# Weight units split four units ahead of use, and a timetable of its own for the second expert's rows

## The chip, the cores and the metric

The kernel runs on one core of a Trainium2 chip. The metric is the device time of one execution in microseconds (us); of several executions the median is taken. TensorE (PE) multiplies matrices, VectorE (DVE) and ScalarE (ACT) work element by element, GpSimd (POOL) issues the gathers and scatters, and SyncE (SP) issues most of the other DMAs. Each engine runs its own program strictly in order, and so does each issuing queue: an instruction that waits holds up all that stand behind it on its engine.

## What is computed

The reference chains three stages. Attention is a retention: 8 batches, 8 heads, 576 tokens, head dimension 64, with scores multiplied by a decay. Its output, 4608 tokens of 512, goes through a mixture of 8 experts of which each token takes one, and the sum through an MLP with a squared ReLU.

```python
# attention
scores = scale * np.matmul(q, k.transpose(0, 1, 3, 2))
ret = scores * Dmat[None, :, :, :]
return np.matmul(ret, v)
...
# mixture of experts: w1[e] is 512 x 1024, w2[e] 1024 x 512
expert_idx = np.argmax(x @ w_gate, axis=1)
for e in range(E):
    mask = expert_idx == e
    h = np.maximum(x[mask] @ w1[e], 0.0)
    out[mask] = gate_w[mask, None] * (h @ w2[e])
...
# MLP: 512 -> 2048 -> 512
r = np.maximum(x @ w_in, 0.0)
return (r * r) @ w_out
```

## The kernel before

**Stages.** Attention runs over 36 tiles of 128 tokens to about 160 us. Then come the experts to about 600 us, and then the MLP, as products of Strassen's kind. The change lies in the stage of the experts.

**Units.** Every expert has 640 places for rows, in CT = 5 tiles of 128. Its hidden layer is cut into 8 slices of 128, and one slice of one expert is a unit: u = 8e + f, 64 units in all (NU). Products are made exact enough by splitting each operand into a high and a low half and adding three products: high by high, low by high, high by low. For a unit, `first(u)` multiplies the expert's rows (`xt`, two halves) by the slice of w1 into a PSUM tile `l` (L813 to L815; three buffers of `l1_ps`); `finish_part` makes from it hh, the high half of the ReLU, on ACT (L819) and hl, the low half, on DVE (L820). `second(u)` multiplies hh and hl by the slice of w2 into accumulators `acc` (L837 to L839). `first` has two parts. For expert 0 these are the lead (tiles 0 and 1, 256 columns, matrix `lead`) and the rest (384 columns); for the others columns 0 to 320 and 320 to 640, which the texts here call a and b. The lead part of units 0 to 5 (MORE = 6) and its `second` are worked off ahead of the loop. So units 0 to 5 are short there: three tiles, 384 columns.

**The loop.** For u from 0 to 63 the body issues loads and what else unit u has to do, then first(u + 1), then second(u). PE is thus one `first` ahead of its `second`. The order in which the calls stand in the body is the order on every engine; no scheduler moves anything.

**Weights.** `load_unit(v)` loads the 512 KB of a unit into `raw` (SP, L106; a pool `stg` of two buffers, so that a load waits until the split of two units before has read its raw). `split_unit(v)` makes the high half on ACT (L112) at once and returns a function that makes the low half on DVE (L114). In iteration u of before, unit u + 7 is loaded and unit u + 6 (AHEAD = 6) is split, near the start of the body.

**Rows of the next expert.** They are fetched tile by tile in four steps, each on its own engine: `gather` (POOL, into `row`, two buffers), `drop` (SP, L778, the tile to a DRAM buffer `r_d`), `lay` (SP, L783, four DMAs of 64 KB that read it back in another layout into `xs`) and `transp` (DVE transposes `xs` into `xf`, L793; ACT makes xt's high half, L797; DVE its low half, L798). A table gives for each step and tile the distance d at which it happens, where d = 0 is the first unit of the expert before: GATHER, DROP, LAY, TURN. Negative numbers reach into the unit group two experts before. For expert 1 there is no such group, so its first steps are written out by hand: gathers of tiles 0 and 1 ahead of the loop, drops of 0 and 1 and the gather of 2 in unit 0, the drop of 2 in unit 1.

**The jobs.** From unit 5 on most units carry a piece of the MLP's preparation (`work`). In `split_wide`, the kind that units 5 and 7 carry, `words` works on a loaded `craw` (SP, L128): ACT size (L141) and four DVE operations (L142 to L152). After the unit's `first` follow ACT cw (L177) and DVE L158, and at the start of the next unit `last_job` issues DVE L180 and L181, and the put, a DMA of 512 KB from cw to `ws_d` (SP, L182). In unit 5, `gate_of` (L295 to L301, five small DVE operations and one of ACT) stands between the two.

**Order in the body.** The load of raw, the load of craw, the end of the last job with its put, the split of u + 6 (high half; the low half is deferred into `rests`), then the steps of the next experts' rows (lay before drop before gather, logits, `transp` with its low half into `rests`), then one of `rests`, the job's `words`, the others of `rests`, then first(u + 1), the job's middle, second(u).

Of the kernel before, what the change touches and what calls it, by code (L numbers as in the profile page):

```python
# [26 lines left out]
FIN = 6  # L27
LEAD = 2
MORE = 6
GATHER, DROP, LAY, TURN = (-3, -2, -1, 1, 2), (-1, 0, 1, 3, 4), (0, 1, 2, 4, 5), (2, 3, 4, 5, 6)  # L30
TINY = 2.0 ** -15 * 1.125
GROUPS = [(0, 8), (8, 16), (16, 24), (24, 30), (30, 36)]

# [17 lines left out]
def body(ctx, tc, att, tab_v, tab_x, masks, wg, ident, pick, cst, wu, wd, out):  # L51
    nc = tc.nc
    vec, act, pe, pool, sp = nc.vector, nc.scalar, nc.tensor, nc.gpsimd, nc.sync
# [9 lines left out]
    w_a = scope(ctx, "w_a", 4, side="right")  # L63
# [40 lines left out]
    def load_unit(u, on=None):  # L104
        raw = on.tile([128, CT, 4, 128], F32, tag="xs", name="raw").rearrange("p a b c -> p (a b c)")[:, 0:1024] if on else pools["stg"].tile([128, 1024], F32, tag="raw", name="raw")
        sp.dma_start(out=raw, in_=wu[u])  # L106
        return raw

    def split_unit(u, raw, on):

        w = ring(u).tile([128, 2, 1024], F32R, tag="w", name="w")
        act.activation(out=w[:, 0], in_=raw, func=AF.Copy)  # L112
        w_q[u] = w
        return lambda: on.tensor_tensor(out=w[:, 1], in0=raw, in1=w[:, 0].bitcast(F32), op=ALU.subtract)  # L114
# [196 lines left out]
    def stream(on, n=None):  # L311

        n = len(ring_q) if n is None else n
        w = on.tile([128, 4, 2, 256], F32R, tag="w", name="wq")
        sp.dma_start(out=w.rearrange("p k s n -> p k (s n)").bitcast(F32), in_=ws_d[stream_of[n]])
        ring_q[n] = w
# [7 lines left out]
    with ExitStack() as es:  # L324
# [278 lines left out]
        raw = {}  # L603
# [89 lines left out]
    NU = NE * 8  # L693
# [56 lines left out]
    with ExitStack() as es:  # L750
# [6 lines left out]
        def gather(e, tiles):  # L757
            for i in tiles:
                j = CT * e + i
                if e == 0:  # L760
                    fetch_rows(xs_t[e][:, i].rearrange("p q c -> p (q c)"), x_d[:, :], gidx[:, j:j + 1])
                    continue
                whole[e, i] = row_p.tile([128, 512], F32, tag="row", name="row")
                fetch_rows(whole[e, i], x_d[:, :], gidx[:, j:j + 1])
# [11 lines left out]
        def drop(e, i):  # L776
            row = whole.pop((e, i))
            sp.dma_start(out=r_d[CT * e + i - CT], in_=row)  # L778
# [6 lines left out]
        def transp(e, i):  # L785
            xs = xs_t[e]
            hi, lo = [a[:, :, 128 * i:128 * i + 128] for a in xt_t[e]]
            if e == 0:
                src = acc_b.tile([128, 4, 128], F32, tag=f"acc{i}", name=f"acc{i}")
                turn_rows(src, xs[:, i].rearrange("p q c -> p (q c)"))  # L790
            else:
                src = xf_p.tile([128, 4, 128], F32, tag="xf", name="xf")
                vec.transpose(  # L793
                    out=src.rearrange("f k (t i) -> f k t i", i=32),
                    in_=xs[:, i].rearrange("q t (k j) -> q k t j", k=4),
                )
            act.activation(out=hi, in_=src, func=AF.Copy)  # L797
            return lambda: vec.tensor_tensor(out=lo, in0=src, in1=hi.bitcast(F32), op=ALU.subtract)  # L798
# [134 lines left out]
            )  # L933

        x0_t, x0_c = [], {}
        AHEAD = 6
        tiles = range(LEAD)
        first(0, (0,))
        fold()
# [46 lines left out]
        raw, made, wide, last_job = {}, [], [], None  # L986
# [19 lines left out]
                        totals += [("sum", work[u][1], r) for r in range(2)]  # L1006
                    break
        assert not ins and not outs and not totals
        raw[AHEAD] = load_unit(AHEAD)
        transp(0, 2)()  # L1010
        first(5, (0,))
        transp(0, 3)()
# [7 lines left out]
        for u in range(NU):  # L1020
            e, f = divmod(u, 8)
            v = u + AHEAD + 1
            if v < NU:
                raw[v] = load_unit(v)
            if u + 1 in work:
                what, j, r = work[u + 1]
                if what != "sum":
                    wide.append(load_wide(2 * j + r, 0 if what == "in" else 1))
            v = u + AHEAD
            job, rests = None, []  # L1030
            if last_job:
                f_ = next(last_job)
                if f_:
                    f_()
                last_job = None
            if v in raw:
                rests.append(split_unit(v, raw.pop(v), vec))
            if u in work:
                what, j, r = work[u]
                if what == "in":  # L1040
                    job = narrow(wide.pop(0), ("ca", "cb")[r], made)
                elif what == "sum":
                    job = left_factors(j, *made[2 * j:], r)
                else:
                    job = split_wide(2 * j + r, wide.pop(0))
            if v == NU + 2:
                assert not last_job and not wide
                early.close()
                w_d = scope(late_es, "w_d", 4, side="right", reuse="tile")
                x0_p = scope(late_es, "x0_p", 1, side="right", reuse="tile")  # L1050
            if v in (NU, NU + 1):
                stream(w_a, 4 + v - NU)
            if v >= NU + 2:
                stream(w_d, v - NU - 2)
            for n, d in ((e + 1, f), (e + 2, f - 8)):
                if n >= NE:
                    continue
                if n == 1 and d == 0:
                    drop(1, 0)
                    drop(1, 1)  # L1060
                    gather(1, [2])
                if n == 1 and d == 1:
                    drop(1, 2)
                if d == 0:
                    places_for(n)
                for i in range(CT):
                    if d == LAY[i]:
                        lay(n, i)
                    if d == DROP[i] and (n, i) in whole:
                        drop(n, i)  # L1070
                    if d == GATHER[i]:
                        gather(n, [i])
                if 1 <= d <= CT:
                    logit(n, d - 1)
                if d in TURN:
                    rests.append(transp(n, TURN.index(d)))
            for f_ in rests[:1]:
                f_()
            if job:
                next(job)  # L1080
            for f_ in rests[1:]:
                f_()
            if u == NU - 3:
                with tc.block():
                    tc.mark_branch_hint_location("rest", "LikelyTaken", [mybir.EngineType.PE])
            if u + 1 < NU:
                first(u + 1, (1,) if u + 1 < MORE else (0, 1))
            if f == 5:
                gate[e] = gate_of(sm, lg_t.pop(e), CT)
            if job:  # L1090
                next(job)
                last_job = job
            if u < NU - FIN:
                second(u, range(LEAD if u < MORE else 0, CT))
                if f == 7:
                    finish(e)
# [407 lines left out]
```

## Time and profile before

| what | us |
|---|---|
| median of 3 runs | 1361.5 (1359.88 to 1361.81) |
| the profiled execution's own time | 1361.44 |
| its span | 1359.7 |
| PE busy | 1340.3 |
| DVE, ACT, POOL busy | 832.9, 546.8, 257.8 |

The span is the stretch that the profiler's records cover, 1.7 us less than the time of the same execution. In the profile, "busy" is the time in which an engine executes, and the idle time ahead of an instruction is put down to whatever released it last. Granted clock is the speed at which PE was allowed to run, 1.00 for the full one. A unit of expert 1 takes PE about 6.9 us.

### The profile page before, as it was taken

What the parts mean: (1) busy time and instruction counts of PE and PEld (TensorE: products, weight loads), DVE (VectorE), ACT (ScalarE), POOL (GpSimd) and SP (SyncE); (2) the same over time, 40 slices, a digit from 0 to 9 for tenths busy, and PEclk for the clock granted to TensorE, in tenths of its full rate; (3) what the DMA queues carried; (4) which work ended last, traced back from release to release, by engine and by line L of the source; (5) the groups of instructions that cost most, each with busy time, mean ns of one, the idle gap of its engine ahead of it and who ended that gap; (6) DMA issues with size and microseconds to landing.
All of it is one profiled execution on the core that took longest, in us unless ns stands there. A gap on an engine that the chain in (4) does not pass through costs nothing.

```text
span 1359.7 us, 21532 instructions
## 1 busy us (share of the span) xinstructions
PE 1340.3 (99%) x8113; PEld 1154.0 (85%) x8113; DVE 832.9 (61%) x1510; ACT 546.8 (40%) x1064; POOL 257.8 (19%) x261
## 2 busy tenths in 40 slices
PE   8999999999999999999999999999999999999998
PEld 6888888999999999989888888888888888888887
DVE  5888757788797888727764563346633566244422
ACT  1232334454455554515544443344423444244321
POOL 2243252240432423112220030001300012000000
PEclk9999999999999999999999999999999999999999
DMA  9999668788978878576865666666656666565562
GB/s 348 350 341 324 198 180 270 257 274 264 302 262 281 283 240 281 194 268 237 294 239 199 226 226 216 216 224 197 243 208 234 209 227 228 203 217 194 191 233 103
DMA packets 129936, 329.10 MB, mean 242 GB/s; under 512 B 20382, under 2 KB 73630, under 8 KB 107808
## 3 DMA queue, kind: packets, MB, share of 16 engines
q1 hardware_dynamic: 121632, 306.51, 65.8%
q0 software_dynamic: 8192, 21.15, 5.3%
q8 instruction: 65, 1.06, 0.3%
q14 instruction: 47, 0.39, 0.1%
HBM read 266.89 MB, written 61.75 MB: 242 GB/s over the span
## 4 chain that ended last, share of the span: by engine, by line
PE 85%; issue 6%; DMA 5%; DVE 2%; SPq 1%; ACT 1%; POOL 1%; POOLq 0%; DVEq 0%; ACTq 0%
PE b L1168 24%; PE fa L1241 10%; PE fa L1240 10%; PE fa L1242 10%; PE l L813 4%; PE l L814 4%; PE l L815 4%; PE acc L837 4%; PE acc L838 4%; PE acc L839 4%; PE x L435 2%; PE sc L383 2%; PE x L431 2%; PE stp L407 1%; DMA idn<-ident 1%
## 5 line engine op out<-in xcount | busy, mean ns | idle before, releaser
L1168 PE MATMUL b<-xt,wq 128*128 128x512 f32 (+1 forms) x1296 | 264.8, 362 | 2.4 <-ACT xt L742 0.7
L1168 PEld LDWEIGHTS b<-xt,wq 128*128 128x128 f32 x1296 | 221.0, 188 | 41.3 <-ACT xt L742 1.1
L1240 PE MATMUL fa<-wq,ch 128*128 128x512 f32 x576 | 224.1, 389 | 0.0
L1242 PE MATMUL fa<-wq,cl 128*128 128x512 f32 x576 | 224.1, 389 | 0.0
L1241 PE MATMUL fa<-wq,ch 128*128 128x512 f32 x576 | 224.1, 389 | 0.0
L1230 DVE TENSOR_TENSOR cl<-g,ch 128x512 fp32r<-128x512 f32 (+1 forms) x160 | 108.6, 687 | 175.3 <-ACT ch L1229 172.9
L1229 ACT ACTIVATE ch<-g 128x512 fp32r<-128x512 f32 (+1 forms) x160 | 91.5, 584 | 183.5 <-PE fa L1241 183.5
L813 PE MATMUL l<-xt,w 128*128 128x320 f32 (+1 forms) x480 | 150.0, 313 | 2.3 <-DVE hl L820 2.3
L814 PE MATMUL l<-xt,w 128*128 128x320 f32 (+1 forms) x480 | 150.0, 312 | 0.0
L815 PE MATMUL l<-xt,w 128*128 128x320 f32 (+1 forms) x480 | 149.9, 312 | 0.0
L733 POOL TENSOR_TENSOR xsum<-yf 128x256 f32<-128x256 f32 x80 | 63.7, 805 | 452.4 <-DVE yf L721 388.7
L837 PE MATMUL acc<-w,hh 128*128 128x512 f32 x320 | 126.3, 395 | 1.3 <-ACT hh L819 1.1
L1242 PEld LDWEIGHTS fa<-wq,cl 128*128 128x128 f32 x576 | 108.1, 188 | 22.6 <-DVE cl L1230 0.2
L1240 PEld LDWEIGHTS fa<-wq,ch 128*128 128x128 f32 x576 | 108.1, 188 | 22.4
L1241 PEld LDWEIGHTS fa<-wq,ch 128*128 128x128 f32 x576 | 108.1, 188 | 22.4
L839 PE MATMUL acc<-w,hl 128*128 128x512 f32 x320 | 125.2, 391 | 0.7 <-DVE hl L820 0.7
L838 PE MATMUL acc<-w,hh 128*128 128x512 f32 x320 | 125.8, 393 | 0.0
L1154 ACT ACTIVATE s<-b 128x512 f32<-128x512 f32 (+1 forms) x120 | 66.5, 555 | 104.9 <-PE b L1168 104.9
L819 ACT ACTIVATE hh<-l 128x320 fp32r<-128x320 f32 (+2 forms) x128 | 54.5, 434 | 127.2 <-PE l L815 104.8
L1189 DVE TENSOR_TENSOR s<-s,s 128x512 f32<-128x512 f32 (+1 forms) x40 | 25.5, 638 | 113.6 <-ACT s L1154 113.6
L813 PEld LDWEIGHTS l<-xt,w 128*128 128x128 f32 x480 | 90.7, 189 | 5.0 <-DVE hl L820 2.5
L814 PEld LDWEIGHTS l<-xt,w 128*128 128x128 f32 x480 | 90.8, 189 | 2.5 <-DVE xt L798 0.2
(177 smaller groups left out, 2083.4 us busy)
## 6 DMA issues: line engine op xcount, KB each, us to landing
wq<-ws_d SPq DMA_DIRECT2D x142, 1024.0 KB
raw<-wu SPq DMA_DIRECT2D x62, 512.0 KB
in<-att SPq DMA_DIRECT2D x28, 1024.0 KB
craw<-wd SPq DMA_DIRECT2D x32, 512.0 KB
ws_d<-cw SPq DMA_DIRECT2D x24, 512.0 KB
x_d<-xr SPq DMA_DIRECT2D x72, 128.0 KB
r_d<-row SPq DMA_DIRECT2D x35, 256.0 KB
xs<-r_d SPq DMA_DIRECT2D x140, 64.0 KB
```

What stands on the lines that cost most here:

```text
L813: pe.matmul(ps, w[:, 0, k], hi[:, k, cs], start=(k == 0), stop=False)
L814: pe.matmul(ps, w[:, 0, k], lo[:, k, cs], start=False, stop=False)
L815: pe.matmul(ps, w[:, 1, k], hi[:, k, cs], start=False, stop=(k == 3))
L837: pe.matmul(acc[i], hh[:, cs], w[:, 0], start=(f == 0), stop=False)
L838: pe.matmul(acc[i], hh[:, cs], w[:, 1], start=False, stop=False)
L839: pe.matmul(acc[i], hl[:, cs], w[:, 0], start=False, stop=(f == 7))
L1168: pe.matmul(ps, w[:, a, c], xc[T][i, b][c], start=(i in (5, 1, 4) and m == 0), stop=(m == 5), skip_group_check=True,)
L1229: act.activation(out=hi[:, o], in_=s, func=AF.Copy)
L1230: vec.tensor_tensor(out=lo[:, o], in0=s, in1=hi[:, o].bitcast(F32), op=ALU.subtract)
L1240: pe.matmul(acc[i], hi[:, cs], w[:, 0], start=(f == 0), stop=False)
L1241: pe.matmul(acc[i], hi[:, cs], w[:, 1], start=False, stop=False)
L1242: pe.matmul(acc[i], lo[:, cs], w[:, 0], start=False, stop=(f == 15))
```

## The change

The four lists become a table STEPS with a row of lists for n = 1 (expert 1) and one with the old numbers for all the others. For expert 1 tiles 0 and 1 are still gathered ahead of the loop; the drops are at d = 0, 1, 2, 4, 5, the lays at 1, 2, 3, 5, 6 and the transposes at 3, 4, 5, 6, 7. The steps written out by hand for expert 1 go. AHEAD becomes 4: iteration u loads unit u + 5 and splits unit u + 4. The load ahead of the loop goes, and so do those of iteration 0, since units 0 to 5 have their weights by other ways (unit 5 among them). In iterations 1 to 4 (u + 1 < MORE) the split, with its low half at once, follows first(u + 1) instead of standing near the start; first(u + 1) and its hh and hl then stand ahead of it. From iteration 5 on it stands where it stood. The conditions near the end of the loop are written in u instead of v and mean the same units. No instruction is added or taken away. Lines of the changed kernel up to the loop have numbers 3 higher.

```diff
-GATHER, DROP, LAY, TURN = (-3, -2, -1, 1, 2), (-1, 0, 1, 3, 4), (0, 1, 2, 4, 5), (2, 3, 4, 5, 6)
+STEPS = {
+    1: ((-1, -1, 1, 2, 3), (0, 1, 2, 4, 5), (1, 2, 3, 5, 6), (3, 4, 5, 6, 7)),
+    2: ((-3, -2, -1, 1, 2), (-1, 0, 1, 3, 4), (0, 1, 2, 4, 5), (2, 3, 4, 5, 6)),
+}
...
-        AHEAD = 6
+        AHEAD = 4
...
-        raw[AHEAD] = load_unit(AHEAD)
...
             v = u + AHEAD + 1
-            if v < NU:
+            if 6 <= v < NU:
                 raw[v] = load_unit(v)
...
-            if v in raw:
+            if v in raw and u + 1 >= MORE:
                 rests.append(split_unit(v, raw.pop(v), vec))
...
             for n, d in ((e + 1, f), (e + 2, f - 8)):
                 if n >= NE:
                     continue
-                if n == 1 and d == 0:
-                    drop(1, 0)
-                    drop(1, 1)
-                    gather(1, [2])
-                if n == 1 and d == 1:
-                    drop(1, 2)
+                gathers, drops, lays, turns = STEPS[min(n, 2)]
...
-                    if d == LAY[i]:
+                    if d == lays[i]:
                         lay(n, i)
...
             if u + 1 < NU:
                 first(u + 1, (1,) if u + 1 < MORE else (0, 1))
+            if v in raw and u + 1 < MORE:
+                split_unit(v, raw.pop(v), vec)()
```

**SP's queue, units 1 to 7.** `raw<-wu` is a unit's load, `r_d<-row` a drop, `xs<-r_d` the four pieces of a lay, `craw<-wd` and `ws_d<-cw` the job's load and put. Before, from the drop of tile 3 to the second job's load:

```order
L778 DMA r_d<-row 128x512
L106 DMA raw<-wu 128x1024
L128 DMA craw<-wd 128x1024
L783 DMA xs<-r_d 32x4x128 x4
L778 DMA r_d<-row 128x512
L106 DMA raw<-wu 128x1024
L783 DMA xs<-r_d 32x4x128 x4
L106 DMA raw<-wu 128x1024
L128 DMA craw<-wd 128x1024
L182 DMA ws_d<-cw 128x1024
L106 DMA raw<-wu 128x1024
L128 DMA craw<-wd 128x1024
```

and in the changed kernel, from the first job's load on:

```order
L131 DMA craw<-wd 128x1024
L781 DMA r_d<-row 128x512
L109 DMA raw<-wu 128x1024
L786 DMA xs<-r_d 32x4x128 x4
L781 DMA r_d<-row 128x512
L109 DMA raw<-wu 128x1024
L131 DMA craw<-wd 128x1024
L185 DMA ws_d<-cw 128x1024
L786 DMA xs<-r_d 32x4x128 x4
L109 DMA raw<-wu 128x1024
L131 DMA craw<-wd 128x1024
```

The last `xs<-r_d`, that of tile 4, stood ahead of the put with two loads between, and stands right behind it now.

**ACT's program, units 1 to 5.** hh and w are numbered by tile; hh_2219, hh_2246, hh_2287, hh_2332 and hh_2401 are those of units 0, 1, 2, 3 and 4, `w<-raw` is a split's high half, xt0 xt's high half. Before:

```order
L819 ACTIVATE hh_2219<-l1_2505 128x384
L112 ACTIVATE w_2522<-raw_2443 128x1024
L819 ACTIVATE hh_2246<-l1_2536 128x384
L112 ACTIVATE w_2565<-raw_2520 128x1024
L819 ACTIVATE hh_2287<-l1_2577 128x384
L112 ACTIVATE w_2603<-raw_2563 128x1024
L797 ACTIVATE xt0_2528<-xf_2612 128x4x128
L819 ACTIVATE hh_2332<-l1_2617 128x384
L112 ACTIVATE w_2643<-raw_2601 128x1024
L797 ACTIVATE xt0_2528<-xf_2647 128x4x128
L819 ACTIVATE hh_2401<-l1_2652 128x384
```

and in the changed kernel:

```order
L822 ACTIVATE hh_2219<-l1_2503 128x384
L822 ACTIVATE hh_2246<-l1_2522 128x384
L822 ACTIVATE hh_2287<-l1_2560 128x384
L822 ACTIVATE hh_2332<-l1_2594 128x384
L115 ACTIVATE w_2609<-raw_2549 128x1024
L800 ACTIVATE xt0_2518<-xf_2630 128x4x128
L822 ACTIVATE hh_2401<-l1_2634 128x384
L115 ACTIVATE w_2649<-raw_2584 128x1024
L800 ACTIVATE xt0_2518<-xf_2667 128x4x128
L822 ACTIVATE hh_2450<-l1_2671 128x384
```

The high halves of units 1 to 3 each stood behind a split, and that of unit 3 behind the first transposed tile as well; now all four follow on one another, and unit 4's is the first with a split ahead of it.

**DVE's program, units 6 and 7.** The L793 (L796) are transposes, L114 (L117) a split's low half, L798 (L801) xt's low half, L820 (L823) hl, the cv rows the next job's words. Before, from the end of the first job:

```order
L180 TENSOR_TENSOR cv_2732<-cv_2732,cw_2780 128x512
L181 TENSOR_TENSOR cw_2780<-cv_2732 128x512
L793 STREAM_TRANSPOSE xf_2801<-xs_2530 128x512
L114 TENSOR_TENSOR w_2799<-raw_2717,w_2799 128x1024
L798 TENSOR_TENSOR xt1_2529<-xf_2801,xt0_2528 128x4x128
L820 SCALAR_TENSOR_TENSOR hl_2809<-l1_2810,hh_2808 128x256
L820 SCALAR_TENSOR_TENSOR hl_2809<-l1_2825,hh_2808 128x384
L114 TENSOR_TENSOR w_2859<-raw_2792,w_2859 128x1024
L142 SCALAR_TENSOR_TENSOR cv_2865<-size_2866,craw_2794 128x512
L146 TENSOR_SCALAR cv_2865<-cv_2865 128x512
L149 SCALAR_TENSOR_TENSOR cv_2865<-cv_2865 128x512
```

and in the changed kernel, from the first row after the same place:

```order
L796 STREAM_TRANSPOSE xf_2787<-xs_2520 128x512
L117 TENSOR_TENSOR w_2781<-raw_2698,w_2781 128x1024
L801 TENSOR_TENSOR xt1_2519<-xf_2787,xt0_2518 128x4x128
L823 SCALAR_TENSOR_TENSOR hl_2795<-l1_2796,hh_2794 128x256
L823 SCALAR_TENSOR_TENSOR hl_2795<-l1_2811,hh_2794 128x384
L796 STREAM_TRANSPOSE xf_2847<-xs_2520 128x512
L117 TENSOR_TENSOR w_2845<-raw_2774,w_2845 128x1024
L145 SCALAR_TENSOR_TENSOR cv_2854<-size_2855,craw_2776 128x512
L149 TENSOR_SCALAR cv_2854<-cv_2854 128x512
L152 SCALAR_TENSOR_TENSOR cv_2854<-cv_2854 128x512
L155 TENSOR_SCALAR cv_2854<-cv_2854 128x512
L801 TENSOR_TENSOR xt1_2519<-xf_2847,xt0_2518 128x4x128
```

The transpose of the last tile moved one unit on, from behind the first job's end to behind the two hl of unit 7 and ahead of the second job's words; behind the words stands its xt1 row, which first(8)b needs. The transpose that stands first in the changed order is that of tile 3.

## Rows read from the trace of the kernel before

**Rows 1.** The page, busy us, share of the span and instructions.
```profile
PE 1340.3 (99%) x8113; PEld 1154.0 (85%) x8113; DVE 832.9 (61%) x1510; ACT 546.8 (40%) x1064; POOL 257.8 (19%) x261
```

**Rows 2.** Waits on PE, 177 to 226: us in total, times, longest.
```profile
PE l L813 <- DVE hl L820: 2.3, 1, 2.3
PE acc L837 <- ACT hh L819: 1.1, 1, 1.1
```

**Rows 3.** Windows, PE: length, busy us (instructions), granted clock, DMA share, GB/s.
```profile
198.00:201.00 3.00, 3.00 (x9) 0.50 0.88 298
215.00:218.00 3.00, 3.00 (x11) 0.50 0.33 131
216.00:217.00 1.00, 1.00 (x4) 0.50 0.00 0
```

**Rows 4.** Windows: length; PE, PEld, DVE, ACT, POOL busy; clock, DMA, GB/s.
```profile
192.42:202.61 10.19, 8.38 (x35) 7.04 (x33) 6.44 (x9) 4.49 (x7) 5.95 (x5) 0.83 0.90 260
210.29:221.42 11.13, 8.79 (x40) 7.91 (x39) 10.36 (x22) 5.73 (x12) 1.28 (x1) 0.85 0.60 206
221.42:228.36 6.94, 6.94 (x40) 6.33 (x39) 5.64 (x10) 3.66 (x7) 1.15 (x1) 1.00 0.76 263
228.36:592.00 363.64, 363.64 (x2064) 333.05 (x2063) 291.74 (x519) 175.18 (x304) 106.25 (x92) 1.00 0.81 268
```

**Rows 5.** Timeline, PE: start, duration, operation [idle before and releaser].
```profile
206.12 0.34 PE L813 MATMUL l<-xt,w 128*128 128x384 f32 x1
...
208.21 0.39 PE L837 MATMUL acc<-w,hh 128*128 128x512 f32 x1
...
214.22 0.44 PE L813 MATMUL l<-xt,w 128*128 128x384 f32 x1 [2.34 <-DVE hl L820]
...
223.18 0.31 PE L813 MATMUL l<-xt,w 128*128 128x320 f32 x1
...
224.94 0.39 PE L837 MATMUL acc<-w,hh 128*128 128x512 f32 x1
```

**Rows 6.** Timeline, ACT, unit 3's split and hh.
```profile
193.80 1.06 ACT L112 ACTIVATE w<-raw 128x1024 fp32r<-128x1024 f32 x1 [6.95 <-DMA raw<-wu]
...
195.28 0.47 ACT L819 ACTIVATE hh<-l 128x384 fp32r<-128x384 f32 x1
```

**Rows 7.** Timeline, DMA issues by SP: start, time to issue them, queue's line.
```profile
183.29 1.78 SPq L778 DMA_DIRECT2D r_d<-row  x2
186.05 2.73 SPq L783 DMA_DIRECT2D xs<-r_d  x4
188.88 0.38 SPq L106 DMA_DIRECT2D raw<-wu  x1
...
202.75 1.75 SPq L783 DMA_DIRECT2D xs<-r_d  x4
...
209.32 1.75 SPq L783 DMA_DIRECT2D xs<-r_d  x4
...
217.94 0.33 SPq L182 DMA_DIRECT2D ws_d<-cw  x1
```

**Rows 8.** Timeline, DVE, the transposes of tiles 3 and 4.
```profile
208.92 0.71 DVE L793 STREAM_TRANSPOSE xf<-xs 128x512 f32<-128x512 f32 x1 [3.50 <-DMA xs<-r_d]
209.56 1.18 DVE L114 TENSOR_TENSOR w<-raw,w 128x1024 fp32r<-128x1024 f32 x1
210.90 0.69 DVE L142 SCALAR_TENSOR_TENSOR cv<-size,craw 128x512 f32<-128x512 f32 x1 [0.15 <-ACT size L141]
...
213.15 0.68 DVE L798 TENSOR_TENSOR xt<-xf,xt 128x512 fp32r<-128x512 f32 x1
...
217.18 0.69 DVE L181 TENSOR_TENSOR cw<-cv 128x512 fp32r<-128x512 f32 x1
...
220.11 0.88 DVE L820 SCALAR_TENSOR_TENSOR hl<-l,hh 128x256 fp32r<-128x256 f32 x2
```

**Rows 9.** Waits of SP's queue, 178 to 226.
```profile
SPq L182 <- DVE cw L181: 5.9, 1, 5.9
```

More of the change, by code (lines that the diff above doesn't have):

```diff
@@ L1045, in body @@
                     job = split_wide(2 * j + r, wide.pop(0))
-            if v == NU + 2:
+            if u == NU - 4:
                 assert not last_job and not wide
@@ L1050, in body @@
                 x0_p = scope(late_es, "x0_p", 1, side="right", reuse="tile")
[L1051 to L1054, printed above, removed]
+            if u in (NU - 6, NU - 5):
+                stream(w_a, 10 + u - NU)
+            if u >= NU - 4:
+                stream(w_d, u + 4 - NU)
             for n, d in ((e + 1, f), (e + 2, f - 8)):
@@ L1066, in body @@
                 for i in range(CT):
-                    if d == LAY[i]:
+                    if d == lays[i]:
                         lay(n, i)
-                    if d == DROP[i] and (n, i) in whole:
+                    if d == drops[i]:
                         drop(n, i)
-                    if d == GATHER[i]:
+                    if d == gathers[i]:
                         gather(n, [i])
@@ L1074, in body @@
                     logit(n, d - 1)
-                if d in TURN:
-                    rests.append(transp(n, TURN.index(d)))
+                if d in turns:
+                    rests.append(transp(n, turns.index(d)))
             for f_ in rests[:1]:
```

## The prediction

> **What bounds the kernel now.** I read the page's busy table first: TensorE (PE) is busy for 1340.3 of 1359.7 us [rows 1]. An edit that leaves PE's instructions alone can give back no more than PE's idle time, plus whatever a lowered clock costs behind an idle stretch. So the next view was the list of waits on PE in the stretch that the diff touches. Its two longest there are 1.1 us on the high half of h, which ScalarE (ACT) makes, and 2.3 us on the low half, which VectorE (DVE) makes [rows 2]. The windows then price them. From 192.42 to 202.61 us PE worked through a first(4), a second(3) and a first(5); undisturbed that is 2.09 + 2.08 + 2.09 = 6.26 us (both lengths from the starts at 206.12 and 208.21 and the window's edge at 210.29 [rows 4, 5]), so **3.9 us** were lost, of which 1.8 idle (10.19 - 8.38). From 210.29 to 221.42 PE did one full unit, 6.94 us undisturbed: **4.2 us** lost, 2.3 of them idle [rows 4]. The rest, about 2 us each time, is the clock: 0.50 in 198 to 201 and in 215 to 218, the lower of the two levels, each time after PE had idled [rows 3]. From 221.42 to 592 PE is at 100% and clock 1.00 [rows 4]. Hence 8.1 us are to be had, and all of it between 192 and 222.
>
> Why these two? **Stall 1**: ACT stood 6.95 us for a raw weight unit until 193.80, with hh of unit 3 behind the split in its program; hh came at 195.28 instead of when PE was done [rows 6]. The load had gone out at 188.88, behind drops and lays on SyncE (SP) [rows 7]. **Stall 2**: DVE stood 3.50 us for lay(1,3) until 208.92, and then the transpose, a split, the words of the wide job and xt's low half came ahead of the hl that PE wanted; PE resumed at 214.22 [rows 5, 8].
>
> **The change part by part.** No operation is added or removed; the order alone moves, in units 0 to 8 and 56 to 60.
>
> *Splits after first() in units 1 to 4.* This takes raw's landing out of hh's way: hh(3) and hh(2) now stand ahead of any split, and hh(4) waits for a split whose load goes out behind a single drop. Stall 1 goes; I count 3.9 us back. Then PE would start first(4) at 192.42, first(5) at 192.42 + 2.09 + 2.08 = 196.59 and end it at 198.68; first(8), which has two parts a and b, would start at 213.30 and part b at 215.06, 8.1 us ahead of the 223.18 of before [rows 5].
>
> *Rows of expert 1 two to three units later than before.* Tiles 0 to 3 are transposed in units 3 to 6; tile 2, the last that first(8)a needs, is done some 5 us ahead of it by the times below. The late one is tile 4, at unit 7, and first(8)b needs it: it covers columns 320 to 640, half of tile 2 and tiles 3 and 4. On SP lay(1,4) now stands **behind the put of cw to ws_d**, which waits for DVE's line 181 of unit 5's job. Before, that put also waited 5.9 us for line 181 [rows 9], but lay(1,4) had left at 209.32, ahead of the put at 217.94 [rows 7]. So the added wait has behind it, on SP, four pieces of lay(1,4); behind them, on DVE, the last transpose; and behind that PE's first(8)b.
>
> When does line 181 end? hh(5) at 198.7, 0.47; split(8) on ACT 1.06, its low half 1.18: 201.4, and the transpose of tile 2 to 202.1. The next load leaves when the low half of split 7 is done (first(4) ends 194.5, and 0.47 + 1.06 + 1.18 to 197.2) and takes 4.92 us as 188.88 to 193.80 did [rows 6, 7]: 202.1. Split 9, 1.06 + 1.18, gives 204.4. From the start of the words to the end of line 181 before took 210.90 to 217.18 + 0.69 = 6.97 us [rows 8]: **211.4**. The queue's own 0.4 us (put 0.33, and 0.07 from 217.87 to 217.94 [rows 7, 8]) brings lay(1,4) out at **211.8**.
>
> How long until it has landed? No row shows a lay behind a put. The long end is 6.17 us (202.75 to 208.92, with the engines busy [rows 7, 8]). At the short end DVE decides: after line 181 it has the transpose of tile 3, a split, xt's low half and two hl, done by 220.11 + 0.88 = 220.99 where line 181 ended at 217.87, so no start before 3.1 us after line 181 [rows 8]. Between them: a drop (same 256 KB) had landed at most 2.76 us after its issue (183.29 to 186.05, where the lay behind it goes out), and the last of four pieces goes out some 1.3 us after the first (1.75 for four) [rows 7], so 4.1. I take 4.2, near the short end, since in 216 to 217 of before, the same place of the program, the DMA engines moved nothing [rows 3]: **216.0**.
>
> The Trainium skill, "DMA: Bandwidth & Descriptors", section "Rules for kernel authors", says to issue a DMA early, compute, and wait on it late; for this one transfer the edit does the opposite. Rows 7 agree, in that the early lay(1,4) cost PE nothing before. The same page, "Anatomy of one DMA — SWDGE (gpsimd) path", puts a transfer at about 2.0 us plus bytes at 436 GB/s, written for the other issuing path; as an estimate a 64 KB piece takes 2.15 us and the lay 1.3 + 2.15 = 3.5, which would bring the end 0.7 us earlier than mine. The 6.17 us of rows 7 and 8 are against it whenever the engines are busy.
>
> From the start of the transpose to the end of xt's low half 4.91 us went by (208.92 to 213.83 [rows 8]), since a split and the words of the next job stand between; the same rows stand between in the changed order. That gives 216.0 + 4.9 = **220.9**, and first(8)b resumes there instead of at 223.18: 2.2 us earlier. PE has then idled for almost 6 us, so I count one stretch at half clock, about 2 us as both stalls of before had (3.9 - 1.8 and 4.2 - 2.3; bounds 0 and 3.9 for none and two). second(7) would start at 220.9 + 1.76 + 2.0 = 224.7, against 224.94 [rows 5]. Net **-0.2 us**: the two stalls turn into one longer one of the same price.
>
> *Elsewhere.* first(7) may wait up to 1 us for the hl behind the words; it lies before the wait of first(8)b and adds nothing. AHEAD 4 for 6 in the middle leaves each engine's order as it is, with every split serving a unit two earlier, still four units (28 us) ahead; the cover is PE's own work, and if a load came 28 us late PE would stall, for which the 364 us without idle [rows 4] give no sign. In units 56 to 60 two more splits fall, 2.2 us of DVE beside 6.9 us of PE each: nothing. Two loads fewer at the end of attention: nothing to 0.25 us gained.
>
> **Rivals.** *All of it comes back* (1361.4 - 8.1 = **1353.4**): lay(1,4) would have to be of no account. For: both stalls' causes are gone. Against: DVE's own rows alone keep xt's last low half from ending before 211.4 + 3.1 + 4.9 = 219.4, 4.3 us after the undisturbed 215.06. *DVE-bound end* (**1357.3 to 1360**): the lay lands within 3.1 us, and the words start up to half a microsecond sooner; first(8)b resumes at 219.0 to 219.4, 3.8 to 4.2 earlier, less 0 to 2 for the clock. For: the idle DMA engines in [rows 3]; against: four small pieces behind a put of 512 KB. *The lay lands late* (slower, **1364.1 to 1366**): after 6.17 us instead of 4.2, with line 181 at 212.4 since the load of unit 9 took 6 us; resumes 212.8 + 6.2 + 4.9 = 223.9, 0.7 later than before, plus 2.0 to 3.9 for the clock. It decides from 5.9 us for the lay if line 181 ends at 212.4 (212.8 + 5.9 + 4.9 = 223.6, +0.4, and a clock price of 2.3 makes it 2.7). The put's 512 KB on the same queue speak for it, the empty engines against. *The edit doesn't do what it says* (**1365**): hh(4) or hh(5) still waits for a load, stall 1 stays at 3.9 us, and everything behind moves: line 181 at 215.3, first(8)b at 224.8, 1.6 later, plus 2. Against: each of the splits now has its load issued some 8 us ahead.
>
> **How the numbers follow.** Chances: my forecast 0.64, all back 0.05, DVE-bound 0.14, lay late 0.12, edit without effect 0.05. The predicted time is the forecast's: the profiled run's 1361.44, which stands within 0.1 us of the median 1361.5, less 0.2: **1361.2**. Its own range is 1359.5 to 1363. The range reaches over the DVE-bound case without its cheapest end, and over most of the late lay: **1358.2 to 1365.0**. A difference of 0.2% (2.7 us) is about what a measurement here tells from no change. Faster by that: all back, two thirds of the DVE-bound case (0.09), and 0.03 of the forecast: 0.17. Slower: most of the late lay (0.10), the edit without effect (0.05): 0.15. The same: 0.68.
>
> **What the profile after would show.** Right: no wait of PE on hh near 195; no stall above 1 us until first(8); one wait of 5 to 6 us on first(8)b, released by xt's low half, ACT or DVE; SP's put before it waiting for line 181 (184 in the new numbering) to about 211.5, lay(1,4) right behind; clock 0.50 for some 3.4 us after it; PE at 100% from unit 8 on. Wrong: if first(8)b waits under 2 us, the lay or DVE was sized too long; if PE idles at 195, the split still blocks hh; if PE has idle time past 230, AHEAD 4 was too short.

## The result

The changed kernel is slower: 1368.7 us median of 6 runs (1366.48 to 1373.62), the kernel before 1361.14 (6 runs, 1359.88 to 1361.81), ratio 1.0060 with a 95% interval of 1.0043 to 1.0077. The profiled execution took 1369.01 us, its span is 1367.2. Forecast were 1361.2 and no change.

PE does the same work in the page of the changed kernel; its idle time grew by 4 us (1367.2 - 1343.8 = 23.4, before 19.4 from [rows 1]), and its busy time by 3.5. Of that 1.4 lie in the first units (47.12 us busy, 45.75 before), where the clock fell behind the stalls below; another part is a stretch at half clock at 9 to 12 us, ahead of anything that the change touches:

```profile
PE 1343.8 (98%) x8113; PEld 1157.0 (85%) x8113; DVE 834.4 (61%) x1510; ACT 544.9 (40%) x1064; POOL 255.1 (19%) x261
```

Four starts on PE cut the program into pieces: second(0), second(8), second(57) and the block of the last six units' second. Their differences, in us, from the timelines of the two traces:

| piece | before | changed | difference |
|---|---|---|---|
| up to second(0) | 181.97 | 180.98 | -0.99 |
| first units, second(0) to second(8) | 49.91 | 55.27 | +5.36 |
| middle, to second(57) | 340.06 | 341.17 | +1.11 |
| last units, to the block | 21.47 | 22.87 | +1.40 |
| the block and the MLP | 766.24 | 766.87 | +0.63 |

The first and the last piece also vary from run to run (second(0) starts between 179.8 and 183.6 in the traces below, of kernels with the same work ahead of it). The other three are the result. In the first units the waits on PE are now these (in us: total, times, longest), against 1.1 and 2.3 of before [rows 2], and 0.7 on hl right behind the 1.1:

```profile
PE l L816 <- ACT xt L800: 3.0, 1, 3.0
PE l L817 <- DVE xt L801: 2.9, 1, 2.9
PE l L816 <- DVE hl L823: 2.2, 1, 2.2
```

The wait on hh at 195 is gone, as intended. The first two rows are one wait on first(8)b, in two steps: the high half of the last tile's xt, then its low half. PE's timeline shows one matmul between:

```profile
218.02 0.31 PE L818 MATMUL l<-xt,w 128*128 128x320 f32 x1
221.35 0.63 PE L816 MATMUL l<-xt,w 128*128 128x320 f32 x1 [3.02 <-ACT xt L800]
224.89 0.63 PE L817 MATMUL l<-xt,w 128*128 128x320 f32 x1 [2.91 <-DVE xt L801]
```

So first(8)b goes on at 224.9, where before it ran at 223.18 [rows 5] after a start of second(0) that was 1 us later. Windows of PE (length, busy, instructions, granted clock, DMA share, GB/s) show what follows, some 6 us at the lower level, where before it was 3 us after each stall [rows 3]:

```profile
225.00:227.00 2.00, 2.00 (x8) 0.50 0.42 131
227.00:229.00 2.00, 2.00 (x8) 0.50 0.00 0
229.00:231.00 2.00, 2.00 (x7) 0.55 0.03 10
```

Where the last tile's xt comes from is read on SP's queue and on DVE. SP's issues (start, time to issue):

```profile
193.40 0.38 SPq L109 DMA_DIRECT2D raw<-wu  x1
196.64 1.75 SPq L786 DMA_DIRECT2D xs<-r_d  x4
198.48 0.39 SPq L109 DMA_DIRECT2D raw<-wu  x1
...
212.92 0.33 SPq L185 DMA_DIRECT2D ws_d<-cw  x1
213.34 3.00 SPq L786 DMA_DIRECT2D xs<-r_d  x4
216.39 0.43 SPq L109 DMA_DIRECT2D raw<-wu  x1
216.86 0.43 SPq L131 DMA_DIRECT2D craw<-wd  x1
```

and DVE's program (the rows that answer to [rows 8]):

```profile
205.89 0.69 DVE L145 SCALAR_TENSOR_TENSOR cv<-size,craw 128x512 f32<-128x512 f32 x1 [0.27 <-ACT size L144]
...
212.17 0.69 DVE L184 TENSOR_TENSOR cw<-cv 128x512 fp32r<-128x512 f32 x1
...
219.92 0.71 DVE L796 STREAM_TRANSPOSE xf<-xs 128x512 f32<-128x512 f32 x1 [3.93 <-DMA xs<-r_d]
...
224.15 0.68 DVE L801 TENSOR_TENSOR xt<-xf,xt 128x512 fp32r<-128x512 f32 x1
```

The chain is the one of the forecast: line 184 ends at 212.86, the put leaves right behind it, lay(1,4) behind the put, the transpose waits for it, and the words stand between the transpose and xt's low half, which ends at 224.83. Counted from second(0), no link came more than 0.1 us earlier than forecast, and two came 2.4 us later.

The 1.4 us of the last units are one wait on hl at 591.08, for which the timelines of ACT, DVE and PE, in this order, give the cause:

```profile
587.48 0.42 ACT L198 ACTIVATE cw<-ca 128x256 fp32r<-128x256 f32 x1 [2.48 <-DMA ws_d<-cw]
587.80 0.62 ACT L202 ACTIVATE cw<-sums 128x512 fp32r<-128x512 f32 x1
588.32 1.05 ACT L115 ACTIVATE w<-raw 128x1024 fp32r<-128x1024 f32 x1
589.27 1.07 ACT L822 ACTIVATE hh<-l 128x320 fp32r<-128x320 f32 x3
```

```profile
589.40 1.22 DVE L117 TENSOR_TENSOR w<-raw,w 128x1024 fp32r<-128x1024 f32 x1 [0.26 <-ACT w L115]
590.54 1.28 DVE L823 SCALAR_TENSOR_TENSOR hl<-l,hh 128x320 fp32r<-128x320 f32 x3
```

```profile
591.08 0.41 PE L816 MATMUL l<-xt,w 128*128 128x320 f32 x1 [1.27 <-DVE hl L823]
```

ACT stands 2.48 us for a put to land, and the last split and three hh queue behind it. These are units in which PE has only first() to do (3.5 us a unit, since the second of the last six units is held back). Before, no split stood there any more, and PE did not wait. The 1.1 us of the middle are a wait of 0.84 us on hl at 540 and what followed it.

### The profile page after: what moved, and what is told of

Its sections match the earlier page's. It is cut to its first block, busy times and chain, and to the rows that moved or that the text cites. A ratio compares the mean times of both kernels' runs of the same rounds, so it can differ in the third digit from the quotient of the medians.

```text
span 1367.2 us, 21527 instructions
## 1 busy us (share of the span) xinstructions
PE 1343.8 (98%) x8113; PEld 1157.0 (85%) x8113; DVE 834.4 (61%) x1510; ACT 544.9 (40%) x1064; POOL 255.1 (19%) x261
## 4 chain that ended last, share of the span: by engine, by line
PE 54%; DMA 1%; ACT 1%; DVE 0%; issue 0%; DVEq 0%
PE b L1167 24%; PE fa L1239 9%; PE fa L1241 9%; PE fa L1240 9%; DMA wq<-ws_d 1%; PE acc L840 0%; PE acc L842 0%; PE acc L841 0%; ACT g L1182 0%; DMA out<-fo 0%; ACT g L1181 0%; DVE xt L749 0%; ACT xt L745 0%; DVE yi L724 0%; DVE xsum L736 0%
## 5 line engine op out<-in xcount | busy, mean ns | idle before, releaser
L822 ACT ACTIVATE hh<-l 128x320 fp32r<-128x320 f32 (+2 forms) x128 | 53.4, 435 | 119.9 <-PE l L818 116.0
```

## Experiments

All times are medians; each ratio is against the kernel before on the same chip, with its 95% interval. Single executions there spread over 1356.5 to 1371.7 us for the kernel before alone, so differences of 2 us are not told apart by the times; the pieces of each trace, in us as in the table above, are. A trace is one execution, though, and not always a middling one: that of fast took 1359.6 us, the shortest of its ten, and that of fast7 1366.5, over 7 us above its median. The ratios are not quotients of the medians shown.

| kernel | time | ratio | first units | middle | last |
|---|---|---|---|---|---|
| before (two traces) | 1361 | | 49.9, 48.5 | 340.1, 340.1 | 21.5, 21.6 |
| changed, first run | 1368.7 | 1.0060 (1.0043 to 1.0077) | 55.3 | 341.2 | 22.9 |
| after_again | 1370.4 | 1.0056 (1.0029 to 1.0083) | 53.9 | 341.5 | 22.9 + 4.4 |
| put_late6 | 1364.1 | 1.0005 (0.9981 to 1.0029) | 51.5 | 340.1 | 23.0 |
| tail6 | 1374.0 | 1.0086 (1.0063 to 1.0108) | 54.3 | 350.9 | 21.5 |
| ahead_only | 1364.2 | 1.0018 (0.9993 to 1.0043) | 50.3 | 341.5 | 23.2 |
| steps_only | 1366.1 | 1.0034 (1.0014 to 1.0054) | 53.4 | 340.9 | 21.5 |
| no_jobs | 1369.2 | 1.0054 (1.0031 to 1.0077) | 45.1 | 346.5 | 22.9 + 4.4 |
| tail4 | 1361.4 | 0.9994 (0.9977 to 1.0010) | 46.4 | 340.1 | 22.9 |
| fast | 1365.6 | 1.0038 (1.0018 to 1.0057) | 45.2 | 344.4 | 21.3 |
| fast6 | 1359.1 | 0.9992 (0.9974 to 1.0010) | 46.6 | 340.2 | 21.6 |
| fast7 | 1359.2 | 0.9986 (0.9964 to 1.0008) | 44.5 | 344.7 | 21.4 + 4.0 |

Without any stall the first units would take 49.9 - 8.1 = 41.8 us, by the forecast's own sum over the trace of before (tail4 and no_jobs, whose first units had no half clock, give 42.6 and 42.7 less their waits). The "+ 4" in the last column is a wait of PE for its own sequencer, of which the last section tells.

**after_again.** No edit: the changed kernel once more.

> The changed kernel once more. Its first profile had one wait of PE at 218 to 225 us on first(8)b (5.9 us idle, second(7) 4.4 us later than before when the low clock is over), and 0.8 and 1.3 us of waits on hl at 540 and 590. Theory 'the order alone makes all three': all three come again in the same units, each within 0.5 us, time 1367 to 1370. Theory 'only the first comes from the order, the two small ones from when transfers happen to land': the wait on first(8)b comes again with 5 to 6.5 us, at least one of the small ones is gone or sits in another unit, time 1365 to 1371.

Both small waits came again at the same places (1.2 us at 538, 1.4 us at 588), and the long one with 7.7 us idle instead of 5.9, more than either theory had allowed. So no piece of the result is an accident of one trace. What differs is the share of half clock: the first units took 53.9 us with more idle time.

**put_late6.** One thing moved:

```diff
             job, rests = None, []
+            put = None
             if last_job:
-                f_ = next(last_job)
-                if f_:
-                    f_()
+                put = next(last_job)
                 last_job = None
+                if put and u != 6:
+                    put()
+                    put = None
...
                 if d in turns:
                     rests.append(transp(n, turns.index(d)))
+            if put:
+                put()
```

> The changed kernel with one thing moved: in unit 6 the four pieces of lay(1,4) go out ahead of the put of cw to ws_d. Theory 'lay(1,4) behind the put makes the long wait': the lay then leaves when its drop has landed, about 211.3 instead of 213.3, and does not share the engines with the put; the last transpose starts at 216 to 217.5 instead of 219.9, first(8)b 2.4 to 3.9 us earlier, so 1363.5 to 1366 against 1368.7, if the clock costs the same. Rival 'DVE's own work between the transposes sets the time': within 1 us of the changed kernel.

SP's issues and DVE's transpose in its trace, where second(0) starts 2.6 us later than in the changed kernel's:

```profile
213.90 1.75 SPq L786 DMA_DIRECT2D xs<-r_d  x4
215.76 0.37 SPq L185 DMA_DIRECT2D ws_d<-cw  x1
```

```profile
219.88 0.71 DVE L796 STREAM_TRANSPOSE xf<-xs 128x512 f32<-128x512 f32 x1 [1.38 <-issue]
```

Counted from second(0) the lay leaves 2.0 us earlier (30.3 against 32.4 us after it), now as soon as its drop has landed, and the first units are 2.4 to 3.8 us shorter than in the two traces of the changed kernel, as expected. So standing behind the put is a good part of the loss, but not all of it. It still took 6.0 us from the first issue to the transpose, with the put behind it instead of ahead. But now a 512 KB load stood ahead of it on the queue: the job's craw, out at 210.82, and by the trace's landing times it took 5.4 us, to 216.2:

```profile
craw<-wd SPq DMA_DIRECT2D x1, 512.0 KB, 5.4
```

So the run shows that the place behind the put sets when the lay leaves. That it has no part in how long the lay then takes is not shown.

**no_jobs.** In units 4 to 7 no craw load, no words, no put:

```diff
-            if u % 8 == 3 and u < NU - 16 or u == 6:
+            if u in (5, 6, 7) or u % 8 == 3 and u < NU - 16 and u not in (11, 19):
                 continue
```

> The changed kernel with no job in units 5 and 7: those two go to units 11 and 19, which carried none, so in units 4 to 7 there are no craw loads, no words and no put. Theory 'put, words and craw loads around lay(1,4) make the long wait long': lay(1,4) leaves when its drop has landed, xt's last low half follows 2.6 us after the transpose starts instead of 4.9, and first(8)b waits 2 to 5 us instead of 5.9 to 7.7; 1361.5 to 1365 against 1368.7 to 1370. Rival 'the row steps alone, gather to lay, are that late': within 1.5 us of the changed kernel.

```profile
PE l L816 <- ACT xt L800: 1.7, 1, 1.7
PE l L817 <- DVE xt L801: 0.6, 1, 0.6
```

These are all its waits on PE from 176 to 240 us. The one on hl at first(7) is gone, and that on first(8)b is 2.4 us instead of 5.9: 45.1 us, 9 to 10 less than the changed kernel. The rest of what made the long wait long is therefore the job: its load ahead of a drop, its words ahead of the low half of xt (which now ends 2.4 us after the transpose starts, and not 4.9), its put; the run doesn't tell the three apart. The lay still took 6.3 us to the transpose (207.58 to 213.92) with no put anywhere near; here a unit's load of 512 KB, out at 205.73, stood ahead of it and landed 5.9 us later, at 211.6. The time as a whole did not follow, since the two jobs went into units 11 and 19, every unit from 8 to 26 then carries one, and PE waited 4.4 us in four pieces on hl between 313 and 346 us (middle 346.5; the granted clock was 1.00 throughout). My expectation of the time had left that out.

**steps_only** and **ahead_only.** The two halves of the change, each put alone into the kernel before: the table STEPS with six ahead and splits as they were, or the splits with the old rows.

```diff
+                gathers, drops, lays, turns = STEPS[min(n, 2)]
```

```diff
-        AHEAD = 6
+        AHEAD = 4
...
+            if v in raw and u + 1 < MORE:
+                split_unit(v, raw.pop(v), vec)()
```

> The kernel before with the new timetable for expert 1 alone; six units ahead and the splits ahead of first(), as before. Theory 'the timetable puts lay(1,4) behind the put and that is what costs': the long wait on first(8)b is there with 4 to 7 us idle, as in the changed kernel, and no wait of more than 0.5 us in units 50 to 59; 1364 to 1368. Rival 'the splits four ahead cost, not the timetable': no wait over 2.5 us at first(8), 1362 or less.

> The kernel before with the splits alone changed (four ahead, in units 1 to 4 behind first()), the rows of expert 1 by the old timetable. Theory 'the splits behind first() take the first stall away and the new timetable is what costs': no wait of PE at 195, lay(1,4) ahead of the put, the wait on hl at first(7) stays at 2 to 5 us; 1358 to 1361.5, with up to 1.4 us lost in the last units. Rival 'the splits four ahead are what costs': 1364 or more.

steps_only has the changed kernel's waits with six units ahead: 

```profile
PE l L816 <- ACT xt L800: 3.7, 1, 3.7
PE l L817 <- DVE xt L801: 3.1, 1, 3.1
PE l L816 <- DVE hl L823: 2.1, 1, 2.1
```

and ahead_only has a single one, 5.9 us on hl at first(7). Each half removes the wait on hh at 195, so they do not add: the second brings nothing that the first has not brought. The timetable alone costs the first units 3.5 to 7 us against the traces of the order of before, and the splits alone 0.4 to 3.9. steps_only came out as its theory said, but for the 0.6 us at 539, and its rival falls. ahead_only's does not: 1364.2 us is what it had named, though the interval reaches down to no change, and with four ahead the last units lose 1.7 us and the middle 1.4 in that trace. Neither half gains anything in the first units: what PE no longer waits at 195 it waits at first(7) or first(8). ahead_only was slower than I expected because the gain of the first stall came back in full in that wait: in its trace DVE stands for lay(1,3) until 207.40, 1.5 us sooner than before [rows 8], of which 1.2 are the earlier start of second(0).

**tail4** and **tail6.** Four ahead in the last units only, in the kernel before, and six ahead again from unit 24, in the changed one.

```diff
-            v = u + AHEAD + 1
+            v = None if u in (35, 43) else u + (7 if u < 35 else 6 if u < 43 else 5)
...
-            v = u + AHEAD
+            v = None if u in (36, 44) else u + (6 if u < 36 else 5 if u < 44 else 4)
```

```diff
+            loads = [u + 5] if u < 23 else [28, 29] if u == 23 else [30, 31] if u == 24 else [u + 7]
...
+            vs = [u + 4] if u < 24 else [28, 29] if u == 24 else [30, 31] if u == 25 else [u + 6]
```

> The kernel before up to unit 34; then the lead of loads and splits falls from six to five (units 35 and 36 skip one) and to four (units 43 and 44), so that the last units are those of the changed kernel. Theory 'four ahead in the last units makes the wait of 1.3 to 1.6 us at 585 to 590': that wait is there, the two stalls at 195 and 212 are as before, 1.3 to 1.9 us slower than before (1362.5 to 1363.5). Rival 'these waits come from when transfers land, after a delay earlier on': none at 585, 0 us.

> The changed kernel, with loads and splits six units ahead again from unit 24 on (two loads and two splits each in units 23 to 25). Theory 'splits in the last units, where PE has only first() to do and takes 3.5 us a unit, make the wait at 590': that wait goes, the one at 218 to 225 stays as it is, 1.3 to 1.5 us faster than the changed kernel. If the wait at 540 belongs to AHEAD 4 too: 2.3 to 2.5 us faster. Rival 'both small waits are a matter of landing times': one of them comes again or sits elsewhere, 0 to 1 us.

tail4 brings the wait in the last units with the rest of the kernel as it was: its one wait on PE from 500 to 604 us, and the same chain on ACT:

```profile
PE l L813 <- DVE hl L820: 1.3, 1, 1.3
```

```profile
580.12 0.42 ACT L195 ACTIVATE cw<-ca 128x256 fp32r<-128x256 f32 x1 [2.48 <-DMA ws_d<-cw]
580.44 0.61 ACT L199 ACTIVATE cw<-sums 128x512 fp32r<-128x512 f32 x1
580.96 1.04 ACT L112 ACTIVATE w<-raw 128x1024 fp32r<-128x1024 f32 x1
581.91 1.07 ACT L819 ACTIVATE hh<-l 128x320 fp32r<-128x320 f32 x3
```

Over all traces the last units take 21.3 to 21.6 us with six ahead and 22.9 to 23.2 with four. That settles the 1.4 us. In the times it does not show (0.9994, where 1.3 us or more had been expected); the interval's upper end, 1.0010, is 1.4 us. tail6 took the wait away (21.5) but was slower as a whole: the two units in which I had it make up two splits also carry jobs, PE waited 3.4 us there and 1.3 to 1.6 us three times later, and the middle went to 350.9. So it tells of the last units and of nothing else.

**fast, fast6, fast7.** Rows of expert 1 as fast as two row buffers allow. All three share the first diff, fast6 and fast7 keep six ahead; fast7 has the second diff too.

```diff
-    1: ((-1, -1, 1, 2, 3), (0, 1, 2, 4, 5), (1, 2, 3, 5, 6), (3, 4, 5, 6, 7)),
+    1: ((-1, -1, 0, 0, 1), (0, 0, 1, 1, 3), (1, 1, 2, 2, 4), (2, 3, 4, 5, 6)),
```

```diff
-            if job:
+            if job and u != 5:
                 next(job)
...
                 first(u + 1, (1,) if u + 1 < MORE else (0, 1))
+            if u == 5:
+                next(job)
```

> The changed kernel's splits with the rows of expert 1 fetched as fast as the two row buffers allow: gathers at d = -1, -1, 0, 0, 1, drops at 0, 0, 1, 1, 3, lays at 1, 1, 2, 2, 4, transposes at 2 to 6; units 6 and 7 loaded ahead of the loop's drops; from units 11 and 19, which carry no job, the splits are five and then six ahead again. Theory 'the rows come late because drops and lays stand behind loads on SP, and that bounds units 6 to 8': lay(1,4) lands near 206 instead of 217, no wait of PE over 1 us between 180 and 230 and none at 590; 6 to 8 us faster than before (1353.5 to 1355.5). Rival 'the engines' work between words and hl bounds it': a wait of 2 to 4 us on first(7) or first(8) stays, 1357 to 1361.

> A version made from what the runs so far show: six units ahead throughout, as before; in units 0 to 5 the split follows first(); the rows of expert 1 as fast as the row buffers allow (drops at 0, 0, 1, 1, 3, lays at 1, 1, 2, 2, 4, transposes at 2 to 6, so that no lay stands behind a put); in unit 4 the job's load goes out ahead of the weight unit's. Theory 'landing times of the rows and words behind a late load are all that bounds units 1 to 8': from second(0) to second(8) PE takes 42 to 44 us (before 46.4 to 49.9, changed kernel 53.9 to 55.3), the rest as before, 3 to 8 us faster than before (1353 to 1358). Rival 'DVE's work between first(6) and first(7) bounds it anyway': a wait of 2 to 3 us on first(7) stays, 45 to 47 us, within 3 us of before.

> The version with six units ahead and fast rows, and in unit 5 the job's words behind first(6) instead of ahead of it, so that hl of first(6) no longer stands behind them on DVE. In the version without this, PE waited 2.2 us for that hl, followed by half clock: 46.6 us from second(0) to second(8). Theory 'the words ahead of hl are the last thing that bounds units 1 to 8': no wait over 0.5 us there, 42 to 43.5 us, and 1354 to 1357 (3 to 6 us faster than before). Rival 'the wait moves on to first(8), since line 184 and the last transpose come later': a wait of 1.5 us or more on first(8), 45 to 47 us, within 2 us of before.

In all three the wait on first(8) for xt is gone, and what is left is a wait on hl: 3.1, 2.2 and 1.4 us, for which DVE stands in the words or in line 184's chain. The first units take 44.5 to 46.6 us, against 46.4 to 49.9 in the three traces with the order of before. So my 42 to 44 for fast6 and 42 to 43.5 for fast7 were too low; fast6's rival came as written, and fast7's nearly so: the wait does move on. fast has its rival's wait, but its median, 1365.6 us, lies above what either theory allowed, and its trace, of the shortest execution, doesn't say where the time went. fast6 and fast7 measure 0.8 and 2.5 us below before, within their intervals; they beat the changed kernel, and a version that clearly beats the kernel before was not found. fast has a wait of 1.9 us at 321 in its middle, a few units after its lead was made up, and fast7 one of 2.9 us at 530, each with half clock behind; their causes were not tried.

**before_again.** The kernel before, for a second trace.

> The kernel before once more, for a second trace of its first units. In its first trace they took 49.9 us from second(0) to second(8), with 4.1 us idle and 4 us of half clock; in the run with four ahead at the end alone, which has the same first units, 46.4 us with 3.8 us idle and no half clock. Theory 'whether a stall of 1.5 to 2.5 us is followed by half clock differs from run to run': a value between 46 and 50 us. Rival 'the change in units 35 to 44 acted on the first units': 49.5 to 50.3 us again.

48.5 us: the same three waits (2.7, 0.7 and 0.9 us), and half clock after the first two only. So the first units of one order spread over 46.4 to 49.9 us with the waits and the clock behind them, and 53.4 to 55.3 us with the new timetable as it stands; the two do not overlap.

## Why the prediction was wrong, step by step

The forecast had the mechanism and priced it too low: two terms of its sum, when the words can start and how long the lay takes to land, were 2.4 us short each. It also missed a second mechanism, in the last units.

- *The first stall goes.* Right: no wait on hh near 195, hh(3) ahead of any split.
- *Line 181 (184) ends at 211.4.* The changed run was 1 us ahead at second(0), so 210.4 in its time; measured 212.86, **2.4 us late**. The words took 205.89 to 212.86 = 6.97 us, as priced, and the load of unit 9 took 4.82 us (forecast 4.92). What failed is its issue: I let it go when the low half of split 7 was done. That half ended at 196.44, but the load stood on SP behind lay(1,2), whose four DMAs went out from 196.64, when its drop had landed, to 198.39; it left at 198.48. I had asked who stands behind the put, and not who stands behind the lays.
- *lay(1,4) lands 4.2 us after its issue.* Measured 213.34 to 219.92, 6.58 us: **2.4 us late**, and past the long end of the bounds too, 3.1 to 6.17. The choice near the short end was wrong. Its reason was that the DMA engines moved nothing in 216 to 217 of before [rows 3]. But a row of before speaks of the order of before. In the changed order two loads leave right behind the lay (216.39, 216.86), and the engines are 0.9 busy:

```profile
216.00:218.00 2.00, 2.00 (x14) 1.00 0.93 257
218.00:221.00 3.00, 0.33 (x3) 0.93 0.91 294
```

  And the put itself moves 512 KB right ahead of the lay on the same queue, for which the sum had no term. The landing times of the put, issued at 212.92, and of the lay's first piece, issued at 213.34, are:

```profile
ws_d<-cw SPq DMA_DIRECT2D x1, 512.0 KB, 4.6
xs<-r_d SPq DMA_DIRECT2D x1, 64.0 KB, 4.4
```

  The put landed at 217.5 and the first piece at 217.7, so 4.2 of the 6.58 us had gone by when the put was down. How the rest divides between the lay's own pieces and the two loads behind it is open. With the put behind and with no put the lay took 6.0 and 6.3 us, each time with a 512 KB load ahead of it instead; no run has this lay without such a neighbour. The rows at hand gave no sure price either. In the first units of before DVE waited for two lays, which took 6.17 us [rows 7, 8] and 6.61 (186.05 to 192.66), while the lay of the 6.17 took 4.08 in tail4, whose order is the same up to unit 34:

```profile
204.53 1.75 SPq L783 DMA_DIRECT2D xs<-r_d  x4
208.61 0.71 DVE L793 STREAM_TRANSPOSE xf<-xs 128x512 f32<-128x512 f32 x1 [1.49 <-DMA xs<-r_d]
```

  The shorter estimate from the Trainium skill, 3.5 us ("DMA: Bandwidth & Descriptors", "Anatomy of one DMA — SWDGE (gpsimd) path", a section on another issuing path), lies further off than 4.2, and the measurement decides. The rule of the same page of the Trainium skill to issue early, do the compute and wait late ("Rules for kernel authors"), which I had set against the change, agrees with the three kernels that lay tile 4 two units earlier: PE waits for no xt in their first units.
- *first(7) may wait up to 1 us, and no stall above 1 us comes until first(8).* Measured 2.2 us, and half clock behind it (0.50 in 211 to 213). It added nothing, as forecast, since DVE, done with both hl of first(7), still stood 3.93 us for the lay.
- *4.9 us from the transpose to xt's low half.* 219.92 to 224.83, 4.91 us: exact.
- *One stretch of half clock, 2 us.* From 224.83 to second(8) at 236.25 are 11.4 us. What PE has to do there is the rest of first(8)b (all but one of its 12 matmuls), second(7) and first(9), and at full clock that takes 1.6 + 3.4 + 3.5 = 8.5. So 2.9 us: 0.9 more.
- *The splits in the last units cost nothing.* Wrong, **+1.4 us**. "6.9 us of PE each" does not hold there: second of the last six units is held back, and PE takes 3.5 us a unit. The cover that I named was half as long, and ACT's wait for the put's landing, in the trace of before as well, stood ahead of the split.
- *AHEAD 4 in the middle changes nothing.* Off by the 0.84 us at 540, but not, or not only, for being four ahead: steps_only has 0.6 us there with six ahead, put_late6 none with four. Why it appears in some orders is open. ACT waits there for a put to land (3.8 us until 533.90 in the changed kernel); that each stall earlier on shifts when puts land is a guess that no run tested.

The sum of the first units: 2.4 + 2.4 + 0.9 late, less the 0.2 us of gain that the forecast had, are 5.5 us, measured 5.36. The rival "the lay lands late" is the case that came (0.12), with its lay and with a late line 181 (by 1 us there, by 2.4 measured), though not with its reason for that: the load took 4.8 us and not 6, it left late. Its 1364.1 to 1366 fall short of 1368.7 by what the last units and the middle added. What should have moved the forecast is that the one term with a wide range had been put near its short end, while the 512 KB ahead of it on the queue stood only among the rivals.

## What to carry to other kernels

A step that is moved behind a queue's waiting entry takes over that wait, and here it landed only after what that entry moved. Before pricing it, walk the whole queue of the changed order, and ask of each entry what it waits for and what it moves, not only of the one that the change names. Two stalls in a row are not two gains: if both feed one chain, removing the first moves its time into the second, as each half of this change did alone. Cover is read where the work will stand: the last units here were half as long as the rest.

## What the runs showed of the hardware

- From the first issue of a lay, four DMAs of 64 KB, to a transpose that waited for it went 4.1 us (tail4, above) to 7.6 (the second trace of before, 183.96 to 191.55). Right behind the put it was 5.7 to 6.7 in four traces (5.74 in steps_only, 6.44 in tail6, 6.58 and 6.74 in the two of the changed kernel).
- Ten of the 13 traces tell when DMAs of SP landed, 1911 of them between 165 and 600 us. As far as these traces tell, all of them landed in the order in which SP issued them.
- A short stall is not always followed by half clock. In tail4 PE waited 1.4 and 0.8 and then 1.6 us and the granted clock stayed at full (so it did in fast behind 3.1 us at first(7)):

```profile
198.00:200.00 2.00, 1.23 (x5) 1.00 0.82 195
200.00:202.00 2.00, 2.00 (x12) 1.00 0.81 255
```

  while before_again, after 2.7 and 0.7 us in the same places, and the kernel before, after 1.1 and 0.7 [rows 2, 3], fell to the lower level. In these traces a stall of 1 to 3 us thus cost itself, or itself and about 2 us more.
- In three of the 13 traces (after_again, no_jobs, fast7) PE waited 4.0 to 4.4 us for its own sequencer ahead of the last units' second, where the others have 0.15 (the row is fast7's):

```profile
597.01 0.47 PE L840 MATMUL acc<-w,hh 128*128 128x512 f32 x1 [4.02 <-PEq L863]
```

  In these three a load of 16 KB of instructions stands inside that wait, 2.7 us before its end; in the other ten it comes 1.2 to 1.5 us after that second has begun. Which of the two brings the other was not tried, nor whether the wait explains the spread of single executions.
